# Spreading the linear layer's token blocks between attention bursts by a credit, and finishing the last block's heads through DRAM

## The chip, the cores and the metric

One core of a Trainium2 chip runs the kernel. The metric is the device time of one execution in microseconds (us); the kernel before takes 2850.27 us, the median of 3 runs (2849.86 to 2850.84). A run of this kernel can be told from no change when it differs by about 0.2%, some 6 us. TensorE does the matrix products, VectorE, ScalarE and GpSimd the element-wise work, and SyncE issues every DMA of this kernel from one queue. A profile calls these engines PE (PEld for its weight loads), DVE, ACT, POOL and SP (SPq for its queue).

## The reference: two pairs of attention layers

The input is 2048 tokens of 576 features. Layer A is attention with 32 query heads of 18 features that share one key and one value head; layer B is linear attention with learned features. They run twice, with the same weights:

```python
x = x + A(layernorm(x)); x = x + B(layernorm(x))
x = x + A(layernorm(x)); x = x + B(layernorm(x))

def A(x):   # multi-query softmax attention
    q = heads(x @ wq); k = x @ wk; v = x @ wv        # 32 x 18 queries, 18 keys, 18 values
    p = softmax(einsum("bhqd,bkd->bhqk", q, k) * 18**-0.5)
    return merge(einsum("bhqk,bkd->bhqd", p, v)) @ wo

def B(x):   # linear attention, 32 heads of 18
    q, k, v = split(x @ wqkv)
    phi = lambda t: concat(softmax(t @ w_phi), softmax(-t @ w_phi))      # 36 features a head
    kv, z = einsum("bhsf,bhsd->bhfd", phi(k), v), sum_s(phi(k))
    return merge((phi(q) @ kv) / (phi(q) @ z + 1e-6)) @ wo_b
```

Everything is float32. Since phi(k)ᵀv is a sum over all tokens, layer B can read nothing out before the last token has passed through layer A.

## The kernel before

**Stages.** The 2048 tokens are 16 blocks of 128. The program is: a setup (layer norm, queries, keys and values of the first layer A); the attention of layer 0; a bridge; the attention of layer 1; and the end. The bridge and the end finish layer B: they mix the blocks that are left, build the state `kvb` (`finish_state`) and read all 16 blocks out (`read_out`, PE line 748); the bridge also prepares the next layer's queries.

**Units.** An attention stage (`attend`) walks through 32 groups, each one block of 128 queries and half of the heads (16). A group has 16 key tiles of 128 keys, and each key tile two units of 8 heads. One unit is two score matmuls (PE line 510) into one of three PSUM tiles, and one exponential over 128 x 1024 (ACT line 988) into one of nine tiles `pt`. So there are 1024 units in a stage. The exponentials of a key tile are then multiplied with the values by four matmuls (PE line 797; the profile shows each in two passes, so 8 per key tile), summed in a PSUM bank over the group. Two banks take turns: one holds the group's sum, the other is the only spare bank, and everything else that PE does in the stage goes through it, one product at a time.

**The rest of a group.** After its last key tile `finish_group` divides by the denominators on DVE (`turned`, `osb`, `parts`, lines 907 to 915, 133 and 134) and writes the heads to DRAM (`keep_group`, `od<-parts`, 8 DMAs, line 829). After a block's second group `load_heads` reads all heads back, transposed (`on<-od`, 4 DMAs, lines 834 and 835).

**The filling work.** For each finished block `stream` gives PE two output projections (14 matmuls of 128 x 288 each, line 240; weights `wo`, input `on`), DVE adds them to the residual (`xc`, line 297), and the block is stored (`xd<-xc`). `flip_tokens` then normalizes it and sends it through DRAM to transpose it (`flipped<-pht`, `xn<-flipped`), and `split_tokens` makes `xs` of it (DVE lines 133 and 134, 664, 665). With `xs`, `mix` runs six more such projections (keys twice, values twice, queries twice, with feature maps on DVE and an exponential on ACT, line 550), and the state update (`update_state`, 32 small matmuls, line 587). So a block is 8 projections and one state update.

**The order of the work** on PE and DVE in the stage is that in which the loop at the end of `attend` records it; a list of dependencies pins it. One turn of the loop is: three units of scores, all value products that are ready, three units of scores, then one projection out of `stream` (`fill`), and again the ready value products unless the filling was long. Where `stream` waits (it sets `st["idle"]`), the loop goes in steps of two units and one key tile. A `tick` moves the generators of DVE work and weight loads one step on.

**The end of a stage.** `last_group` normalizes the last group, and `pack` moves its heads from `parts` into the transposed place `on` by 22 DMAs inside SBUF (lines 853, 856). Both output projections of block 15 wait for that. After it, all of block 15's layer norm follows, and `last_mix` mixes the blocks of `st["left"]`: three in layer 0, two in layer 1. The weights `wpq` for their queries are read again from DRAM, since the room that held them in the stage is gone.

Of the kernel before, what the change touches and what calls it, by code (L numbers as in the profile page):

```python
# [61 lines left out]
def kernel(ctx, tc, x_in, wq, wk, wv, wo, wqkv, w_phi, wob, out):  # L62
# [185 lines left out]

    def run(gen):
        for _ in gen:  # L250
            pass
# [50 lines left out]
    def fold_phi(ps, tmp):  # L302
# [33 lines left out]
        short(ps.tile([P, P], F32, name="ps"), st)  # L336
        yield -110
        for n, (half, k) in enumerate(units):
            following = fetch(n + 1)
            pt = ps.tile([P, 4, P], F32, name="ps")  # L340
# [4 lines left out]
            po = ps.tile([P, 504], F32, name="ps")  # L345
# [5 lines left out]
            pl = ps.tile([P, 2 * P], F32, name="ps")  # L351
# [210 lines left out]
    def keys_values(i, xs, e, st, ps, copies):  # L562
        vb = st["vb"][i % 2]
        for b in range(2):
            po = ps.tile([P, HALF], F32, name="ps")
            yield from project(po, st["wk"], b * HALF, xs, lambda: feature_start(heads(po), e, b, copies))
# [10 lines left out]
        for b in range(2):  # L577
            po = ps.tile([P, HALF], F32, name="ps")
            yield from project(po, st["wv"], b * HALF, xs, lambda: values(po, b))
        return vb  # L580

    def update_state(e, vb, st, ps, after=None):
        phi = e.rearrange("p h s d -> p (h s d)")
        pk = ps.tile([P, SG * 2 * DH], F32, name="ps")
# [13 lines left out]
    def queries(xs, e, st, ps, copies):  # L598
        for b in range(2):
            po = ps.tile([P, HALF], F32, name="ps")  # L600
            yield from project(po, st["wpq"], b * HALF, xs, lambda: feature_start(heads(po), e, b, copies))
# [44 lines left out]
    def flip_tokens(i):  # L646
        rstd, bias = ln_stats([i])[i]
        xn = bw.tile([P, H, 2, DH], F32, name="featq").rearrange("p h s d -> p (h s d)")[:, :D]
        V.tensor_scalar(xn, xres[i], rstd, bias, op0=ALU.mult, op1=ALU.add)
        blocks = bw.tile([P, NKG, P], F32, name="pht").rearrange("p a b -> p (a b)")  # L650
        run(block_transpose(blocks[:, :D], xn, flipped[i]))
# [16 lines left out]
    def mix(i, xs, st, ps, spill, loads, slow, after):  # L668
        ek, eq = (bw.tile([P, H, 2, DH], F32, name=tag) for tag in ("featk", "featq"))
        vb = yield from keys_values(i, xs, ek, st, ps, V)  # L670
# [10 lines left out]
    def last_mix(n, i, stats, st, sp, ps, spill):  # L681
        xn = layer_norm(i, stats, bw if n % 2 else sp, A, "xn" if n % 2 else "xo")
        yield STAGE
        xs = bw.tile([P, 9, P], F32R, name="xs") if n % 3 == 0 else sp.tile([P, 9, P], F32R, name="xs3")
        yield from transposed(xn, xs, ps, A, LOE)
        yield STAGE
        if n % 2:
            ek, eq = (bw.tile([P, H, 2, DH], F32, name=tag) for tag in ("featk", "featq"))
        else:
            both = sp.tile([P, 9, PW], F32, name="xsc").rearrange("p a b -> p (a b)")  # L690
            ek, eq = (both[:, k * 2 * D : (k + 1) * 2 * D].rearrange("p (h s d) -> p h s d", s=2, d=DH)
                      for k in range(2))
        vb = yield from keys_values(i, xs, ek, st, ps, A)
        yield STAGE
        if n < 2:
            yield from queries(xs, eq, st, ps, A)
# [3 lines left out]
        if n >= 2:  # L700
# [3 lines left out]
        pht = sp.tile([P, NKG, P], F32, name="phs", bufs=1)  # L704
# [35 lines left out]
    def read_out(i, pht, st, sp, ps):  # L740
# [22 lines left out]
        for b in range(2):  # L763
            po = ps.tile([P, HALF], F32, name="ps")
# [72 lines left out]
    def load_first_heads(on, c):  # L837
        src = ods[c % 2]
        for n in range(2):
            nc.sync.dma_start(on[:, 5 * n : 5 * n + 2, :], src[n, : 2 * P].rearrange("(k p) t -> p k t", p=P))  # L840
            nc.sync.dma_start(on[:32, 5 * n + 2, :], src[n, 2 * P : 2 * P + 32])

    def pack(dst, src, g):
        for j in range(GH):
            for x in range(HS):
                row, cols = (first_head(g, j) + x) * DH, slice(x * P, (x + 1) * P)
                d0 = 0
                while d0 < DH:
                    k, r = divmod(row + d0, P)
                    n = min(DH - d0, P - r)  # L850
                    rows = slice(32 * j + d0, 32 * j + d0 + n)
                    if k < 4:
                        nc.sync.dma_start(dst[r : r + n, k : k + 6 : 5, :], src[rows, :, cols])  # L853
                    else:
                        for half in range(2):
# [546 lines left out]
```

## Time and profile before

| | before |
|---|---|
| median of 3 runs | 2850.27 us |
| the profiled execution | 2848.92 us, of it the span 2847.1 us |
| PE / PEld busy | 2667.7 us (94%) / 1474.3 us (52%) |
| ACT busy | 2147.3 us (75%), 1920.1 us of it exponentials of scores |
| DVE / POOL busy | 1249.2 us (44%) / 61.6 us (2%) |
| DMA | 251.81 MB, mean 88 GB/s |
| mean granted clock of PE | 0.968 |

A row of the timeline has a start in us, a duration, the engine, the source line, the operation, output and input, and how many such instructions were merged; in brackets stands the idle time of the engine before it and what ended that. PE's rows overlap, because matmuls are pipelined, so the distance from the start of one group of scores to the next is the better measure of what a burst costs. In the view of waits a row says who waited for whom, how long in total, how often, and the longest. A table by stretches gives the busy time of each engine in each of them, the granted clock, the share of the DMA engines and GB/s.

### The profile page before, as it was taken

Reading aid. Unit: us, or ns where it says so; the run is one execution under the profiler, and the core shown is the slowest. Engines: PE = TensorE matmul, PEld = TensorE weight load, DVE = VectorE, ACT = ScalarE, POOL = GpSimd, SP = SyncE. Lnnn points to the kernel's source line nnn. Section 1 sums busy time; section 2 is a strip of 40 time slices with the busy share of each in tenths; the row PEclk is TensorE's granted clock in tenths of the full one; section 3 lists DMA queues with packets and bytes.
Section 4 is the critical chain, followed back from the end, with each engine's and each line's share of the span. In section 5 each row is a group of like instructions: output and inputs, shape, how many; then the busy total and the mean of one; then the engine's idle time right before and its main releaser. Section 6 shows DMA issues by size and latency. Waiting matters only on the chain. (4 is left out here: it accounts for less than half of the span.)

```text
span 2847.1 us, 55572 instructions
## 1 busy us (share of the span) xinstructions
PE 2667.7 (94%) x22046; PEld 1474.3 (52%) x22046; DVE 1249.2 (44%) x2852; ACT 2147.3 (75%) x2521; POOL 61.6 (2%) x102
## 2 busy tenths in 40 slices
PE   7999999999999999979999999999999999999799
PEld 6633434444444444538994344444444444444389
DVE  8432144444444444437772233443344443444165
ACT  4699988888988887953337888888888888888621
POOL 1000000000000000002000000000000000000010
PEclk9999999999999999989999999999999999999889
DMA  6463244222222322126546222222221222221164
GB/s 188 149 209 109 64 118 135 56 60 52 60 60 55 73 63 64 48 60 214 176 127 209 57 56 56 56 56 48 51 59 45 54 57 51 56 56 38 40 206 147
DMA packets 472596, 251.81 MB, mean 88 GB/s; under 512 B 216136, under 2 KB 426632, under 8 KB 472328
## 3 DMA queue, kind: packets, MB, share of 16 engines
q1 hardware_dynamic: 472328, 248.17, 31.3%
q8 instruction: 177, 2.90, 0.4%
q14 instruction: 91, 0.75, 0.1%
HBM read 140.90 MB, written 104.63 MB: 86 GB/s over the span
## 5 line engine op out<-in xcount | busy, mean ns | idle before, releaser
L988 ACT ACTIVATE pt<-sc 128x1024 f32<-128x1024 f32 x2036 | 1920.1, 1047 | 310.5 <-PE sc L510 294.6
L510 PE MATMUL sc<-qst,kst 56*128 56x512 f32 x3840 | 703.4, 453 | 24.9 <-ACT pt L988 22.1
L510 PEld LDWEIGHTS sc<-qst,kst 56*128 56x128 f32 x3840 | 322.6, 186 | 574.2 <-ACT pt L988 521.4
L797 PE MATMUL acc<-pt,vst 128*32 128x512 f32 x4096 | 498.6, 602 | 6.1 <-DVE xc L297 3.3
L797 PE MATMUL ps<-pt,vst 128*32 128x512 f32 x4048 | 497.0, 603 | 0.0
L240 PE MATMUL ps<-wahi,xs 128*128 128x288 f32 x1035 | 236.7, 315 | 27.5 <-DVE xs L133 23.7
L797 PEld LDWEIGHTS acc<-pt,vst 128*32 128x32 f32 x4096 | 107.3, 109 | 226.7 <-issue 214.7
L797 PEld LDWEIGHTS ps<-pt,vst 128*32 128x32 f32 x4048 | 105.9, 110 | 215.4 <-issue 210.9
L240 PEld LDWEIGHTS ps<-wahi,xs 128*128 128x128 f32 x1035 | 177.2, 197 | 55.9 <-issue 25.2
L240 PE MATMUL ps<-walo,xs 128*128 128x288 f32 x575 | 174.5, 305 | 0.0
L240 PE MATMUL acc<-wchi,on 128*128 128x288 f32 x477 | 115.4, 327 | 34.8 <-DMA on<-od 33.9
L297 DVE TENSOR_TENSOR xc<-xc,acc 128x288 f32<-128x288 f32 x53 | 23.9, 451 | 252.8 <-PE acc L240 252.8
L240 PEld LDWEIGHTS acc<-wchi,on 128*128 128x128 f32 x477 | 83.2, 202 | 59.5 <-issue 25.9
L240 PEld LDWEIGHTS ps<-walo,xs 128*128 128x128 f32 x575 | 113.6, 198 | 0.0
L388 PE MATMUL ps<-xsc,wbhi 128*128 128x256 f32 x576 | 107.0, 284 | 0.7 <-ACT xsc L131 0.7
L240 PE MATMUL ps<-wbhi,xs 128*128 128x288 f32 x486 | 107.0, 305 | 0.0
L131 ACT ACTIVATE xs<-ps 128x512 fp32r<-128x512 f32 x37 | 22.0, 595 | 107.0 <-PE ps L283 106.9
L574 DVE COPY vb<-ps 128x288 f32<-128x288 f32 x44 | 20.1, 458 | 186.2 <-PE ps L240 186.2
L410 ACT ACTIVATE pc<-ps 128x256 fp32r<-128x256 f32 x80 | 30.5, 385 | 93.6 <-PE ps L388 90.8
L907 DVE STREAM_TRANSPOSE turned<-ps 128x512 f32<-128x512 f32 x32 | 22.9, 717 | 158.4 <-PE ps L797 121.1
L388 PEld LDWEIGHTS ps<-xsc,wbhi 128*128 128x128 f32 x576 | 90.8, 191 | 1.6 <-ACT xsc L131 1.1
L240 PEld LDWEIGHTS ps<-wbhi,xs 128*128 128x128 f32 x486 | 79.6, 188 | 16.1 <-issue 15.7
(263 smaller groups left out, 3034.0 us busy)
## 6 DMA issues: line engine op xcount, KB each, us to landing
qst<-qd SPq DMA_DIRECT2D x360, 72.0 KB
od<-parts SPq DMA_DIRECT2D x496, 36.0 KB
pht<-phi SPq DMA_DIRECT2D x32, 540.0 KB
qd<-pc SPq DMA_DIRECT2D x64, 256.0 KB
phi<-pht SPq DMA_DIRECT2D x108, 144.0 KB
on<-od SPq DMA_DIRECT2D x60, 256.0 KB
xd<-xc SPq DMA_DIRECT2D x33, 288.0 KB
xc<-xd SPq DMA_DIRECT2D x30, 288.0 KB
```

What stands on the lines that cost most here:

```text
L131: A.activation(dst_hi, src, AF.Copy)
L240: T.matmul(dst, xs[:, slot, :], w[half][:, k, c0 : c0 + HALF], start=(n == 0), stop=(n == last))
L297: V.tensor_add(xr, xr, po)
L388: T.matmul(po, lhs, xsc[:, slot, :], start=(n == 0), stop=(n == LASTP))
L410: A.activation(pc[:, 0, :], po, AF.Copy)
L510: T.matmul(sc, kst[head_rows(h), t * P : (t + 1) * P], q[head_rows(h), h // 2, :], start=True, stop=True)
L574: V.tensor_copy(dst, heads(po))
L797: T.matmul(acc[32 * j : 32 * j + 32, :], vst[:, t, :], pts[j], start=first, stop=last)
L907: V.transpose(turned, acc[c, g])
L988: A.activation(pt, sc, AF.Exp, scale=SCALE)
```

## The change

**Pacing.** `bankful` lets `stream` say what its next product is before it takes the spare bank: a projection ("P"), a state update ("U") or a piece of the weights' folding ("F"). `peek` runs `stream` up to there. Each burst of three units earns credit (`PACES`: 0.6 a burst while layer 0's weights are folded, then 0.44; 0.39 in layer 1; at most 2 are held). A projection takes the place of a burst's value products, costs one credit, and never comes in two bursts in a row. Otherwise the burst has two or three key tiles of value products, and a state update stands behind them.

**A block early.** `hooks` record the layer norm's statistics and the flip of the next block between the value projections of the present one, and `turn_tokens` records its `xs` split behind the state update. `wanted` lets a block's mix start only when the output of the following block is done. `flip_tokens` normalizes in place in `xres[i]` now. After `load_heads` there are four steps of waiting instead of three.

**The end of a stage.** Two blocks are left in either layer, 14 and 15. Block 14's `last_mix` is recorded in pieces between those of `last_group`, so all its projections stand ahead of block 15's output projections. The last group's heads go the way of all others: `keep_group` to DRAM, and `load_part` back. `pack` is gone, and the order of `wo` and `wpq` in the rooms is exchanged, so that `wpq` stays to the end and is not read again.

```diff
+    def bankful(kind, ps, shape=(P, HALF)):
+        yield Kind(kind)
+        return ps.tile(list(shape), F32, name="ps")
...
-    def flip_tokens(i):
-        rstd, bias = ln_stats([i])[i]
-        xn = bw.tile([P, H, 2, DH], F32, name="featq").rearrange("p h s d -> p (h s d)")[:, :D]
-        V.tensor_scalar(xn, xres[i], rstd, bias, op0=ALU.mult, op1=ALU.add)
+    def flip_tokens(i, stats):
+        rstd, bias = stats[i]
+        V.tensor_scalar(xres[i], xres[i], rstd, bias, op0=ALU.mult, op1=ALU.add)
...
-    def pack(dst, src, g):
...
+    def load_part(on, c, g):
+        src, edge = ods[c % 2], HG * DH - 2 * P
+        for n in range(2):
+            k = 5 * n
+            if g == 0:
+                nc.sync.dma_start(on[:, k : k + 2, :], src[n, : 2 * P].rearrange("(k p) t -> p k t", p=P))
+                nc.sync.dma_start(on[:edge, k + 2, :], src[n, 2 * P : 2 * P + edge])
+            else:
+                nc.sync.dma_start(on[edge:, k + 2, :], src[n, 2 * P + edge : 3 * P])
+                nc.sync.dma_start(on[:, k + 3, :], src[n, 3 * P : 4 * P])
+                nc.sync.dma_start(on[n * 64 : n * 64 + 64, 4, :], src[n, 4 * P :])
...
-            pack(on.bitcast(F32), parts.bitcast(F32), NG - 1)
+            keep_group(parts.bitcast(F32), c, NG - 1)
+            load_part(on.bitcast(F32), c, NG - 1)
...
-                    for _ in range(3):
+                    for _ in range(4):
...
+            def burst():
+                ready = scores(BURST)
+                tick()
+                earn(BURST)
+                work = peek()
+                held = at[0] + BURST - 2 * done[0]
+                if work == "P" and credit[0] >= 1 and not paused[0] and held <= TILES:
+                    fill()
+                    credit[0] -= 1
+                    paused[0] = True
+                else:
+                    paused[0] = False
...
+                    count = 3 if credit[0] + st["pace"] >= 1 else 2
+                    sums(min(ready, max(done[0] + count, -(-(at[0] + BURST - TILES) // 2))))
+                    if work == "U":
+                        fill()
+                    tick()
...
                 if not st["idle"]():
-                    sums(scores(BURST))
-                    tick()
-                    ready = scores(BURST)
-                    spent = fill()
-                    in_order()
-                    opens = done[0] < len(units) // 2 and units[2 * done[0]][1] == 0
-                    if spent < HEAVY and not (spent and opens):
-                        sums(ready)
-                    tick()
-                    tick()
+                    burst()
...
+    PACES = ((0.6, 0.44), (0.39, 0.39))
...
-            on, c = st["on"], NT - 1
-            last_group(st["last"], on, ps)
-            EARLY, LATE = range(6), range(6, len(PRODUCTS))
...
+                on = st["heads_in"]()
+                load_part(on.bitcast(F32), c, 0)
+                ahead = last_mix(left[0], ln_stats(left[:1]), st, bw, ps, spills[layer])
+                closing = last_group(st["last"], on, c, ps, tail)
...
+                for job in (ahead, closing, ahead, closing, ahead, ahead):
+                    advance_to(job)
+                for b in range(2):
+                    po = ps.tile([P, HALF], F32, name="ps")
+                    run(project(po, st["wo"], b * HALF, on))
+                    add_residual(c, b, po)
```

**DVE at the opening of a mix, layer 1.** The order before, from the flip of a block to the first copy of its keys; `turned`, `osb` and the `parts` belong to a group that ends in between:

```order
L639 STREAM_TRANSPOSE pht<-featq 128x576
L907 STREAM_TRANSPOSE turned<-ps 128x512
L911 RECIPROCAL rd<-turned 128x16
L912 TENSOR_TENSOR turned<-turned,rd 128x512
L915 STREAM_TRANSPOSE osb<-turned 128x512
L133 CAST parts<-osb 128x512
L134 TENSOR_TENSOR parts<-osb,parts 128x512
L133 CAST xs<-xn 128x512
L134 TENSOR_TENSOR xs<-xn,xs 128x512
L664 CAST xs<-xn 128x128
L665 TENSOR_TENSOR xs<-xn,xs 64x128
L543 COPY featk<-ps 128x16x18
```

The four rows `xs<-xn` were the last thing ahead of the first key copy: the key projection that it copies had to wait for them. In the change the same four rows stand behind the state update (`kv<-kv,acc`) of the block before, ahead of the rest of the group's end:

```order
L551 COPY featq<-ps 128x16x18
L553 TENSOR_REDUCE fmax<-featq 128x16
L554 TENSOR_REDUCE fmin<-featq 128x16
L555 TENSOR_TENSOR featq<-fmin,featq 128x16x18
L556 TENSOR_TENSOR featq<-featq,fmax 128x16x18
L908 STREAM_TRANSPOSE turned<-acc 128x512
L603 TENSOR_TENSOR kv<-kv,acc 128x288
L133 CAST xs<-xn 128x512
L134 TENSOR_TENSOR xs<-xn,xs 128x512
L673 CAST xs<-xn 128x128
L674 TENSOR_TENSOR xs<-xn,xs 64x128
L912 RECIPROCAL rd<-turned 128x16
```

Between these rows and the first key copy of that block now lie two output projections and five to eight more bursts.

**PE around a state update, layer 1.** Before, from the burst behind the last query projection to the first output projection (`acc<-wchi,on`):

```order
L510 MATMUL sc<-qst,kst 128x512 x6
L797 MATMUL ps<-pt,vst 32x512 x12
L510 MATMUL sc<-qst,kst 128x512 x6
L587 MATMUL acc<-featk,vb_17415 32x36 x32
L797 MATMUL ps<-pt,vst 32x512 x4
L510 MATMUL sc<-qst,kst 128x512 x6
L797 MATMUL ps<-pt,vst 32x512 x8
L510 MATMUL sc<-qst,kst 128x512 x6
L240 MATMUL acc<-wchi,on 128x288
```

In the change, the same place:

```order
L518 MATMUL sc<-qst,kst 128x512 x6
L806 MATMUL ps<-pt,vst 32x512 x12
L597 MATMUL acc<-featk,vb_17365 32x36 x32
L518 MATMUL sc<-qst,kst 128x512 x6
L806 MATMUL ps<-pt,vst 32x512 x4
L518 MATMUL sc<-qst,kst 128x512 x4
L806 MATMUL ps<-pt,vst 32x512 x4
L518 MATMUL sc<-qst,kst 128x512 x6
L806 MATMUL ps<-pt,vst 32x512 x8
L518 MATMUL sc<-qst,kst 128x512 x6
L240 MATMUL acc<-wdhi,on 128x288
```

A two-unit step (scores x4) and its key tile now stand in addition between the group's end and the first product that needs `on`.

**PE behind the last value products of layer 1.** Before, with `acc<-pt,vst` the last products, lines 866 and 873 the transposes of `last_group`, then block 15's output:

```order
L797 MATMUL acc<-pt,vst 32x512 x12
L866 MATMUL ps<-idf,xn 128x128 x4
L873 MATMUL ps<-idf,featk 128x128 x4
L240 MATMUL ps<-wchi,on 128x288
L240 MATMUL ps<-wclo_17979,on 128x288
```

In the change (`osb` and `wide` are `last_group`'s, `xn` and `xs` are block 14's):

```order
L806 MATMUL acc<-pt,vst 32x512 x8
L864 MATMUL ps<-idf,osb 128x128 x4
L290 MATMUL ps<-idf,xn 128x128 x4
L294 MATMUL ps<-idf,xn 128x128
L873 MATMUL ps<-idf,wide 128x128 x4
L240 MATMUL ps<-wahi,xs 128x288
L240 MATMUL ps<-walo,xs 128x288
```

Block 14's six projections (84 matmuls) and its state update come next, and only then block 15's output projections.

More of the change, by code (lines that the diff above doesn't have):

```diff
@@ L1366 @@
             order = range(NT)
-            jobs = [last_mix(n, i, stats, st, sp, ps, spills[layer]) for n, i in enumerate(left)]
+            st["sp"] = sp
+            jobs = [last_mix(c, stats, st, sp, ps, spills[layer]), ahead]
             jobs += [finish_state(st, sp, ps)]
```

214 lines of the change are left out of this document (112 added, 102 removed).

## The prediction
> **What bounds the kernel now.** I first cut the span into its stages, at the first exponential and at the last value products of either attention stage. The columns are the stretch, its length, the busy time of PE, PEld, DVE, ACT and POOL, the granted clock, the share of the DMA engines and GB/s.
>
> ```profile
> span 2847.1 us, 55572 instructions
> ...
> 110.30:1251.90 1141.60, 1093.37 (x8639) 516.52 (x8639) 466.39 (x947) 996.21 (x1076) 8.12 (x15) 0.98 0.30 83
> 1251.90:1511.00 259.10, 233.96 (x2469) 223.54 (x2467) 173.44 (x511) 80.14 (x186) 25.41 (x34) 0.94 0.52 159
> 1511.00:2680.80 1169.80, 1107.20 (x8637) 517.15 (x8637) 440.40 (x888) 994.07 (x1080) 8.11 (x15) 0.98 0.24 61
> 2680.80:2847.10 166.30, 139.97 (x1604) 132.59 (x1604) 86.00 (x245) 26.28 (x60) 10.47 (x10) 0.89 0.50 153
> ```
>
> Two attention stages are 2311 us of 2847. In either ACT has about 995 us of work, so 147 and 176 us are left in which it stands; PE looks busy, but a matmul that is queued behind another counts as busy. What a burst costs is read from the timeline, where the starts of the score groups follow each other:
>
> ```profile
> 1841.39 0.90 PE L510 MATMUL sc<-qst,kst 56*128 56x512 f32 x4
> ...
> 1843.22 0.91 PE L510 MATMUL sc<-qst,kst 56*128 56x512 f32 x4
> ...
> 1848.72 2.86 ACT L988 ACTIVATE pt<-sc 128x1024 f32<-128x1024 f32 x3 [2.39 <-PE sc L510]
> ...
> 1858.09 0.96 PE L510 MATMUL sc<-qst,kst 56*128 56x512 f32 x6
> ...
> 1861.04 1.06 PE L510 MATMUL sc<-qst,kst 56*128 56x512 f32 x6
> 1862.03 2.78 PE L797 MATMUL acc<-pt,vst 128*32 128x512 f32 x24
> 1864.74 0.96 PE L510 MATMUL sc<-qst,kst 56*128 56x512 f32 x6
> ```
>
> A burst with a projection takes 2.95 us (1858.09 to 1861.04), of it 1.99 the projection, and one with three key tiles of value products 3.70: the pair is 6.65 us for six units, of which ACT needs 5.7 (two times 2.86). A two-unit step takes 1.83 us. There ACT is the limit: PE's own share is 0.32 for each unit and 0.93 for the key tile, 1.57. So PE bounds the stage where projections stand, ACT where none stand, and PE's idle 0.26 us a step is all that spreading can use.
>
> **Stalls on PE.** The waits of the layer 1 stage (ACT's, then PE's), and an opening of a mix that waits, from the timeline:
>
> ```profile
> ACT pt L988 <- PE sc L510: 167.4, 153, 6.3
> ...
> PE ps L240 <- DVE xs L133: 23.7, 13, 2.8
> PE acc L240 <- DMA on<-od: 17.1, 21, 2.0
> ...
> 1913.03 0.91 PE L510 MATMUL sc<-qst,kst 56*128 56x512 f32 x4
> ...
> 1917.32 0.37 PE L240 MATMUL ps<-wahi,xs 128*128 128x288 f32 x1 [2.38 <-DVE xs L133]
> ...
> 1920.53 1.65 PE L510 MATMUL sc<-qst,kst 56*128 56x512 f32 x6
> ```
>
> This two-unit step with the first key projection takes 7.50 us (1913.03 to 1920.53) where 1.83 + 1.99 = 3.82 would do. DVE reaches `xs` only behind a group's end, as the order of before shows. Of the 15 such openings in layer 1, eleven look like this one and four like the step that began at 1843.22 and ended with this row, 4.89 us later:
>
> ```profile
> 1848.11 0.97 PE L510 MATMUL sc<-qst,kst 56*128 56x512 f32 x6
> ```
>
> That is 11 x 3.68 + 4 x 1.07 = 45 us. The first output projection waits for the heads out of DRAM:
>
> ```profile
> 1884.79 3.28 SPq L829 DMA_DIRECT2D od<-parts  x8
> ...
> 1888.89 0.38 SPq L834 DMA_DIRECT2D on<-od  x1
> ...
> 1890.78 0.97 PE L510 MATMUL sc<-qst,kst 56*128 56x512 f32 x6
> ...
> 1893.29 0.54 PE L240 MATMUL acc<-wchi,on 128*128 128x288 f32 x2 [0.92 <-DMA on<-od]
> ...
> 1895.08 0.97 PE L510 MATMUL sc<-qst,kst 56*128 56x512 f32 x6
> ```
>
> Its burst takes 4.30 instead of 2.95 us, and about 13 of 15 do: 18 us. The trip through DRAM is 8.5 us, from the first issue at 1884.79 to the arrival at 1893.29.
>
> The wait at 1917.32 cost more than itself: 3.68 us were lost with 2.38 us of idle, since the projection took 3.21 us (1917.32 to 1920.53) instead of 1.99. The Trainium skill (TensorE: Matmul & The Clock Gate, What's actually happening) says that an idle window of about 3.4 us halves PE's clock until a busy one has passed. The row agrees in kind with a shorter gap; by the page alone a 2.38 us gap would cost 2.38 us, and the openings 14 us less.
>
> **Layer 1's stage, by bursts.** The order of the change holds the same work, 114 projections and 14 state updates, as 98 pairs (14 of them with a state update), 16 single projection bursts, 61 bursts with two key tiles, 12 with one and 77 two-unit steps. A burst with two key tiles needs 0.96 + 1.85 on PE and 2.86 on ACT, so 2.86; one with one tile 0.96 + 0.93 = 1.89. The state update is
>
> ```profile
> 1885.88 0.75 PE L587 MATMUL acc<-featk,vb 128*32 128x36 f32 x63
> ```
>
> 98 x 6.65 + 14 x 0.75 + 16 x 2.95 + 61 x 2.86 + 12 x 1.89 + 77 x 1.83 = 1048 us, and 15 for the 16 units at the start: 1063. The same sum for before (99 pairs, 15 openings at 3.82, 34 bursts with two tiles, 86 steps, 36 with one tile, 14 state updates, and the start) is 1066. So the spreading by itself gives 3 us; the 104 us by which the stage exceeds its sum are the 45 and 18 of stalls, and 41 of bursts gated by ACT where a feature exponential falls in, and of the start. In the change `xs` is split five or more bursts ahead of its first use, at least 10 us, and `on` has one step of waiting more and a further burst with two key tiles: from `osb` to its first product I count at least four two-unit steps and a burst, 10.2 us, against the 8.5 and some 1.2 of DVE. Both stalls go. What is late next is the gating by ACT: I keep 30 of the 41 (bounds 15 and 50, for new waits too). 1063 + 30 = 1093: **-77 us** (-92 to -57).
>
> **Layer 0's stage.** One block more is mixed here: six projections and a state update, + 6 x 1.99 + 0.75 = 12.7 us, on PE, which bounds it. The stalls that go:
>
> ```profile
> PE acc L240 <- DMA on<-od: 16.8, 11, 4.3
> ...
> PE acc L240 <- DVE featk L543: 5.0, 1, 5.0
> ...
> PE acc L797 <- DVE xc L297: 3.3, 1, 3.3
> ```
>
> 25.1 us of idle, which with the slow clock behind it (3.68 for 2.38) are 39. Six may stay, because weights are stored to DRAM in this stage. -33 + 13 = **-20 us** (-40 to +5).
>
> **The two ends.** The chain of waits behind the last value products of layer 1:
>
> ```profile
> 2680.83 0.70 DVE xn L863
> ...
> 2685.81 0.70 DVE xs L134
> 2686.69 0.76 SPq L856
> ...
> 2702.78 0.70 SPq L856
> ...
> 2706.16 0.88 ACT xo L273
> ...
> 2708.88 10.02 PE ps L240 x56
> 2719.45 3.73 PE ps L240 x28
> ...
> 2744.68 2.53 PE ps L748 x44
> ```
>
> And two rows of DVE's timeline in that stretch:
>
> ```profile
> 2705.55 0.94 DVE L297 TENSOR_TENSOR xc<-xc,ps 128x288 f32<-128x288 f32 x2 [19.05 <-PE ps L240]
> ...
> 2708.37 0.16 DVE L266 SCALAR_TENSOR_TENSOR lnb<-mv,rstd 128x1 f32<-128x1 f32 x1 [0.72 <-POOL rstd L264]
> ```
>
> SP issues `pack`'s 22 DMAs one by one, 17 us, and PE has next to nothing meanwhile; the first read-out comes 63.9 us after the last value products. In the change the normalization takes 5.0 to the first heads (2680.83 to 2685.81) and 1.2 more, for two DVE rows of block 14 stand ahead. Then 8.5 for the trip, and 3 for six more loads at about 0.5 each: `on` is there at 17.7. PE does block 14 in this time: from about 4 us on 84 matmuls, 10.02 + 3.73, and the state update, to 18.5. The output projections 3.7: 22.2. From then on block 15 stands alone: sum and statistics 3.0 (2705.55 to 2708.53), norm and transposes 2.7 (2706.16 to 2708.88), keys and values 8 to 10, state 2, queries 3.7, which makes 43 at the first read-out, and two of doubt for a cold PE: 45, **-19 us** (-24 to -10). The rest of the end is as before.
>
> The bridge starts its read-outs (first start in this row) 73.2 us after its last value products at 1251.9, since it mixes three blocks:
>
> ```profile
> L748 PE MATMUL ps<-kvb,pht x704: 206/222/357, 1325.1 to 1469.8; 108*64 108x57 f32 x160, 72*64 72x38 f32 x16
> ```
>
> In the change the same 45, so -28; up to 3 may be lost where read-outs wait for their output weights, whose 10 DMAs can start only after block 15's keys. **-27 us** (-32 to -15).
>
> A rule against this part: the Trainium skill (DMA: Bandwidth & Descriptors, Anatomy of one DMA) gives every DMA a fixed cost of about 2 us, mostly the receipt of the last write, and a way through DRAM pays it twice where `pack` pays once. By it the ends would be 2 us worse each; the measured trip of 8.5 us holds both.
>
> **The sum.** 2847.1 - 20 - 27 - 77 - 19 = 2704 us of span; 1.8 us lie around it (2848.92), and the median stands 1.4 above this execution: 2707.
>
> **The rivals.** First, the stalls only change their place: each new step of the chain (spare bank, DVE, DRAM) is late elsewhere, so that the stages keep their 104 and about 70 us above the sums. Layer 1 gives 3, layer 0 loses 13; with the ends -46 that is -36: about 2814. For it speaks that the sums of bursts are hardly better; against it, that the waits have known causes, which the order removes. Second, the other side: DVE now meets `xs<-xn` ahead of a group's `turned` and `osb`, and if the block is not back from DRAM, DVE stands, and behind it the group's end, `on`, and the emptying of the spare bank for which PE waits. The price is in this row of all waits:
>
> ```profile
> DVE xs L133 <- DMA xn<-flipped: 25.6, 5, 10.5
> ```
>
> 28 flips at 10.5 us are 294 us, against -143: 3001. It turns the sign from 5.1 us a flip on, just this row's mean. Against it: from flip to split lie two pairs and a state update, over 13 us, and the row has five waits in 27 flips of before. Third, ACT-gating goes too, because PE always has something in hand: the stages reach their sums and layer 0 loses all its idle, 1063 and about 1100: 2850.3 - 107 - 42 - 48 = 2653. The bursts next to two-unit steps speak against it.
>
> **How the numbers follow.** 0.70 for the forecast, 0.12 for the first rival, 0.05 for the second, 0.11 for the third, 0.02 for no change at all or less. The terms' bounds, which will not all fall on one side, make 2675 to 2745; a part of the first and third rival makes the range 2662 to 2770. Faster by over 0.2% is 0.94, slower 0.05.
>
> **What would show it.** Right: the layer 1 stage takes 1078 to 1113 us, its waits of PE for `xs` and for `on` are each under 6 us, ACT's wait for scores falls from 167 to below 110, and the first read-outs come 40 to 50 us after the last value products. The forecast is wrong if the waits vanish and the stage still takes over 1130 (then the sum by bursts is wrong), or if DVE shows long waits for `xn<-flipped` or PE for the spare bank's emptying.

## The result, and the profile after

The changed kernel takes 2770.67 us (median of 4 runs, 2763.83 to 2773.81) against 2850.56 of before on the same chips; the ratio is 0.9715, with an interval of 0.9695 to 0.9735. It is faster by 80 us, where 143 were forecast: the median lies 0.7 us beyond the upper end of the range, and the interval reaches into it. The table by stretches of the profile after, cut at the same events as that of before; a stage begins at its first scores, some 1 us ahead of the first exponential (length, busy time of PE, PEld, DVE, ACT and POOL, granted clock, DMA share, GB/s):

```profile
span 2767.5 us, 55568 instructions
...
110.80:1252.10 1141.30, 1098.64 (x8787) 526.52 (x8787) 488.07 (x988) 1000.57 (x1082) 8.12 (x15) 0.99 0.31 82
1252.10:1480.80 228.70, 217.47 (x2303) 208.46 (x2303) 162.15 (x485) 72.63 (x170) 20.64 (x30) 0.97 0.55 168
1480.80:2617.80 1137.00, 1088.46 (x8637) 517.54 (x8637) 439.27 (x886) 998.93 (x1080) 7.88 (x15) 0.98 0.24 62
2617.80:2767.50 149.70, 132.55 (x1604) 126.51 (x1604) 87.29 (x246) 26.01 (x60) 10.72 (x11) 0.97 0.53 161
```

| stretch | before | forecast | after |
|---|---|---|---|
| layer 0's stage | 1141.6 | -20 (-40 to +5) | 1141.3, -0.3 |
| bridge | 259.1 | -27 (-32 to -15) | 228.7, -30.4 |
| layer 1's stage | 1169.8 | -77 (-92 to -57) | 1137.0, -32.8 |
| end | 166.3 | -19 (-24 to -10) | 149.7, -16.6 |

Both ends came as worked out. The read-outs (first start in the row of either layer) begin 42.8 and 43.8 us behind the last value products:

```profile
L757 PE MATMUL ps<-kvb,pht x704: 206/222/357, 1294.9 to 1439.6; 108*64 108x57 f32 x160, 72*64 72x38 f32 x16
...
L757 PE MATMUL ps<-kvb,pht x704: 206/222/357, 2661.6 to 2754.4; 108*64 108x57 f32 x160, 72*64 72x38 f32 x16
```

What is missing, 64 us, lies in the two attention stages. The waits of layer 1's stage (ACT's, PE's with its weight loads, and DVE's) show where:

```profile
ACT pt L992 <- PE sc L518: 124.7, 145, 6.0
...
PE acc L240 <- DMA on<-od: 29.1, 20, 2.7
...
PEld acc L240 <- DMA on<-od: 13.3, 12, 1.7
...
DVE xs L133 <- DMA xn<-flipped: 3.8, 1, 3.8
```

PE has no wait for `xs` any more (23.7 us before), and DVE's waits for a block on its way back are 3.8 us instead of 25.6. But PE waits for `on` longer than before, 29.1 instead of 17.1 us. One such place, in the timeline:

```profile
1831.01 2.03 SPq L838 DMA_DIRECT2D od<-parts  x1
...
1838.99 1.38 DVE L649 STREAM_TRANSPOSE pht<-featq 128x1152 f32<-128x1152 f32 x1
1840.40 0.31 SPq L652 DMA_DIRECT2D phi<-pht  x1
1840.69 0.96 PE L518 MATMUL sc<-qst,kst 56*128 56x512 f32 x6
1840.88 0.48 SPq L843 DMA_DIRECT2D on<-od  x1
...
1843.97 0.37 PE L240 MATMUL acc<-wdhi,on 128*128 128x288 f32 x1 [2.31 <-DMA on<-od]
1844.17 0.29 PE L240 MATMUL acc<-wdlo,on 128*128 128x288 f32 x1
1845.48 0.85 PE L240 MATMUL acc<-wdhi,on 128*128 128x288 f32 x2 [1.02 <-DMA on<-od]
...
1847.81 0.67 PE L240 MATMUL acc<-wdhi,on 128*128 128x288 f32 x2
1848.29 0.33 PE L240 MATMUL acc<-wdlo,on 128*128 128x288 f32 x1
1848.54 0.96 PE L518 MATMUL sc<-qst,kst 56*128 56x512 f32 x6
```

The last part of the heads is issued to DRAM by 1833.04, and the first of the loads that bring them back starts only at 1840.88, 7.8 us later. Between the two, on SP, stands the first DMA that stores the block's features (`phi<-pht`), and it waits for DVE's transposition, which ends at 1840.37. In the kernel before the load followed at once (1888.89 in the prediction's row, behind eight issues that end at 1888.07). The burst takes 7.85 us (1840.69 to 1848.54) instead of 2.95.

SP's rows of the whole stage show the same order in 13 of 15 blocks. In nine of them the store's data are late, and the load starts 7.8 to 9.6 us behind the last store of heads; in eight of these PE's first product then waits 2.0 to 2.7 us. In the kernel before the store stood there in 6 blocks, and no load started more than 3.1 us behind. The 113 projection bursts of the stage, from one start of scores to the next, take 380 us instead of 113 x 2.95 = 333.

### The profile page after: what moved, and what is told of

It reads as the page before. It is cut to its first block, busy times and chain, and to the rows that moved or that the text cites. A ratio compares the mean times of both kernels' runs of the same rounds, so it can differ in the third digit from the quotient of the medians.

```text
span 2767.5 us, 55568 instructions
## 1 busy us (share of the span) xinstructions
PE 2631.2 (95%) x22030; PEld 1464.7 (53%) x22030; DVE 1259.8 (46%) x2867; ACT 2148.7 (78%) x2511; POOL 56.9 (2%) x98
## 5 line engine op out<-in xcount | busy, mean ns | idle before, releaser
L518 PE MATMUL sc<-qst,kst 56*128 56x512 f32 x3840 | 694.9, 452 | 21.2 <-ACT pt L992 20.9
L240 PE MATMUL ps<-wahi,xs 128*128 128x288 f32 x882 | 193.3, 305 | 0.8 <-ACT xs L131 0.6
L240 PEld LDWEIGHTS ps<-wahi,xs 128*128 128x128 f32 x882 | 145.9, 190 | 11.4 <-issue 7.8
L240 PE MATMUL ps<-walo,xs 128*128 128x288 f32 x490 | 144.6, 297 | 0.0
L240 PE MATMUL acc<-wdhi,on 128*128 128x288 f32 x450 | 110.0, 329 | 32.0 <-DMA on<-od 31.9
L240 PEld LDWEIGHTS acc<-wdhi,on 128*128 128x128 f32 x450 | 79.7, 205 | 51.9 <-issue 32.7
L418 ACT ACTIVATE pc<-ps 128x256 fp32r<-128x256 f32 x80 | 30.4, 384 | 94.4 <-PE ps L396 92.9
L240 PE MATMUL ps<-wbhi,xs 128*128 128x288 f32 x459 | 100.9, 305 | 0.0
L240 PE MATMUL ps<-wchi,xs 128*128 128x288 f32 x432 | 96.0, 308 | 0.0
L240 PEld LDWEIGHTS ps<-walo,xs 128*128 128x128 f32 x490 | 93.3, 190 | 0.0
L396 PE MATMUL ps<-xsc,wblo 128*128 128x256 f32 x320 | 86.5, 286 | 0.0
```

Source lines behind the costliest of these rows:

```text
L240: T.matmul(dst, xs[:, slot, :], w[half][:, k, c0 : c0 + HALF], start=(n == 0), stop=(n == last))
L396: T.matmul(po, lhs, xsc[:, slot, :], start=(n == 0), stop=(n == LASTP))
L418: A.activation(pc[:, 0, :], po, AF.Copy)
L518: T.matmul(sc, kst[head_rows(h), t * P : (t + 1) * P], q[head_rows(h), h // 2, :], start=True, stop=True)
```

## The experiments

Each ran on a chip together with the kernel before, so the ratios are to be compared; one thousandth is 2.8 us. The lengths are read from each run's profile in the same way as above. E1 to E4 start from the changed kernel, E5 to E9 from E1, E10 to E12 are as their texts say.

| run | median us | ratio (interval) | layer 0 | bridge | layer 1 | end | first read-outs |
|---|---|---|---|---|---|---|---|
| after | 2770.7 | 0.9715 (0.9695 to 0.9735) | 1141.3 | 228.7 | 1137.0 | 149.7 | 42.8, 43.8 |
| E1 feature store late | 2712.7 | 0.9539 (0.9518 to 0.9560) | 1132.0 | 229.0 | 1093.4 | 146.8 | 43.5, 43.9 |
| E2 eight steps | 2720.7 | 0.9571 (0.9549 to 0.9593) | 1137.3 | 229.0 | 1086.5 | 155.4 | 43.1, 52.6 |
| E3 guard | 2756.1 | 0.9688 (0.9664 to 0.9711) | 1136.0 | 230.3 | 1133.1 | 152.6 | 42.6, 44.7 |
| E4 block 14 behind | 2785.5 | 0.9800 (0.9777 to 0.9822) | 1138.8 | 236.3 | 1134.4 | 163.9 | 53.4, 62.1 |
| E5 no spreading | 2745.8 | 0.9653 (0.9631 to 0.9675) | 1149.9 | 230.3 | 1104.2 | 150.6 | 42.7, 42.6 |
| E6 split at use | 2726.4 | 0.9586 (0.9566 to 0.9606) | 1139.0 | 229.3 | 1097.2 | 146.0 | 43.4, 43.1 |
| E7 old folding | 2700.7 | 0.9496 (0.9475 to 0.9517) | 1100.5 | 246.8 | 1093.6 | 145.9 | 56.3, 42.8 |
| E8 slower folding | 2723.4 | 0.9573 (0.9551 to 0.9595) | 1144.5 | 229.0 | 1091.3 | 148.9 | 43.4, 44.4 |
| E9 no early flip | 2749.0 | 0.9664 (0.9635 to 0.9692) | 1141.4 | 242.8 | 1089.4 | 158.8 | 52.4, 56.6 |
| E10 old folding, six steps | 2720.0 | 0.9557 (0.9528 to 0.9585) | 1134.6 | 227.3 | 1089.5 | 157.0 | 42.3, 49.3 |
| E11 the same, pace 0.37 | 2714.1 | 0.9544 (0.9515 to 0.9573) | 1134.8 | 228.0 | 1077.8 | 160.9 | 42.3, 57.9 |
| E12 no opening behind | 2749.6 | 0.9667 (0.9651 to 0.9683) | 1112.6 | 228.7 | 1137.8 | 159.7 | 43.0, 57.5 |

**E1, the feature store eight ticks later.**

```diff
-        next(spilling)
-        slow.append(spilling)
+        slow.append(later(spilling))       # later: eight ticks, then the same job
```

> The store of a block's features (phi<-pht) is recorded eight ticks later; PE's order stays the same. Theory A (SP's queue): in the changed kernel on<-od stands on SP behind phi<-pht, which waits for DVE's transposition, so the 12 late output projections of layer 1 cost 78 us instead of 12 x 2.95 = 35. Here on<-od comes ahead of it: PE's wait for on<-od in the layer 1 stage falls from 29 us to under 6, the stage from 1137 to 1095 (1090 to 1105), layer 0's stage stays within 8 us of 1141, the time is about 2728. Theory B (the trip through DRAM is too long for the steps that cover it, whatever SP does): the wait stays over 20 us and the time within 10 us of 2771. Theory C (stalls only change their place): the wait goes, but the stage stays above 1120, with another wait of PE or ACT grown by as much.

The job that is put off holds DVE's transposition as well as the store. Layer 1's stage fell to 1093.4, the ratio by 0.0176, some 50 us. The 113 projection bursts take 337 us instead of 380, and those 43 us are all that the stage lost. PE has no wait for `on` in its list, and the timeline of the same block shows why:

```profile
1817.82 0.38 SPq L847 DMA_DIRECT2D on<-od  x1
...
1826.16 0.40 PE L240 MATMUL acc<-wdhi,on 128*128 128x288 f32 x1
...
1828.20 1.08 PE L518 MATMUL sc<-qst,kst 56*128 56x512 f32 x6
...
1835.35 1.37 DVE L649 STREAM_TRANSPOSE pht<-featq 128x1152 f32<-128x1152 f32 x1
...
1836.75 0.95 SPq L652 DMA_DIRECT2D phi<-pht  x2
```

The load starts 8.3 us ahead of its first product and not 3.1. Theory A holds. PE's order is the same, so the steps were enough to cover the trip through DRAM (against B), and no other wait took its place (against C): ACT's waits for scores fell from 124.7 us too:

```profile
ACT pt L996 <- PE sc L518: 79.2, 134, 5.7
```

**E2, eight steps in place of four.**

```diff
-                    for _ in range(4):
+                    for _ in range(8):
```

> Eight steps instead of four between load_heads and the output projections; this moves also the order of bursts, and on SP on<-od comes ahead of phi<-pht. Theories A and B both let the wait for on<-od go and the layer 1 stage fall to 1090 to 1110; B alone expects this run to gain where the one with the late feature store does not. Theory C keeps the stage above 1120. Layer 0's stage, whose waits for on are 3 us, stays within 10 us of 1141 by all. Time 2720 to 2745 by A and B.

Layer 1's stage is 1086.5. This does not show that more steps cover a late load, since no load is late here: in all 15 blocks it starts 0.8 to 0.9 us behind the last store of heads, ahead of the feature store. Nor is the whole gain one of the stage: two projections moved from it into the end, where the last block is mixed later (first read-out 52.6 us behind the last value products instead of 43.8).

**E3, the guard of the folding.**

```diff
+                    filled = work == "F" and credit[0] >= 1      # ahead of the fill
...
-                    count = 3 if credit[0] + st["pace"] >= 1 else 2
+                    opens = filled and done[0] < len(units) // 2 and units[2 * done[0]][1] == 0
+                    count = 0 if opens else 3 if credit[0] + st["pace"] >= 1 else 2
```

> Behind a folding product no value products that open a new group (the guard that the kernel before had): three bursts of layer 0 change, the rest of PE's order stays. Theory A (the -20 of layer 0 was eaten in the folding, by value products that wait for DVE to empty the bank): the three waits of PE of 2.7, 2.4 and 2.0 us at value products go, with the slow clock behind them 8 to 12 us, so layer 0's stage goes from 1141 to about 1131 and the time to about 2761. Rival (the folding is bound by DVE's copies between its products, PE merely waits for them at another place): layer 0's stage stays within 4 us of 1141. Layer 1 stays at 1137 by both.

Layer 0's stage fell by 5.3 us, half of what theory A wanted; with runs of one kernel 10 us apart that decides nothing by itself. Of the three waits that it was to remove, two went and the one of 2.0 us stayed. This is one of the two, in the changed kernel:

```profile
333.39 0.66 PE L350 MATMUL ps<-idf,wstage 128*126 128x128 f32 x4
...
335.45 0.69 DVE L134 TENSOR_TENSOR parts<-osb,parts 128x512 fp32r<-128x512 f32 x1
336.06 0.68 DVE L351 COPY xn<-ps 126x512 f32<-126x512 f32 x1
...
336.79 1.94 PE L806 MATMUL ps<-pt,vst 128*32 128x512 f32 x8 [2.74 <-DVE xn L351]
```

A folding product sits in the spare bank, DVE has a group's end ahead of the copy that empties it, and the value products behind it need that bank, since they open a new group.

**E4, block 14 behind the last output.**

```diff
-                for job in (ahead, closing, ahead, closing, ahead, ahead):
+                for job in (closing, closing):
```

> Block 14's keys, values and queries go behind block 15's output projections, as in the kernel before; the heads still go through DRAM. Theory A (block 14 fills the 14 us in which PE would wait for the last heads): in either end the first read-out comes 10 to 15 us later (53 to 58 us behind the last value products instead of 43), the time is 2790 to 2800. Rival (block 14's products would lie beside block 15's chain of small steps anyway): the read-outs start within 4 us of 43, the time within 8 us of 2771. The attention stages stay as they are by both.

The first read-outs came 10.6 and 18.3 us later, the second by more than the 15 that theory A allowed, and the ratio rose by 0.0085, 24 us. Block 14's 14 us of products do fill the wait for the last heads; behind block 15's chain they are not hidden.

**E5, no spreading.**

```diff
-    PACES = ((0.6, 0.44), (0.39, 0.39))
+    PACES = ((0.6, 9), (9, 9))
```

> On the kernel with the late feature store (2712.7 us), the pace is so high that credit never holds a projection back behind the folding: projections come in every second burst and the rest of a block's time is two-unit steps, 115 instead of 77 of them in layer 1. Theory A (the sum of bursts decides, spreading by itself is worth 3 us): layer 1's stage by the same prices is 114 x 2.95 + 101 x 3.70 + 14 x 4.45 + 16 x 2.86 + 12 x 1.89 + 115 x 1.83 + 15 = 1066, against 1063, so 1093 becomes 1096 (1086 to 1106), and the time 2712 to 2725. Theory B (spreading is what takes the stalls away): waits for xs and on return, the stage is 1125 or more, the time above 2745.

Layer 1's stage is 1104.2, within theory A's bounds; 4.7 us of it is one wait of value products for DVE. Layer 0's stage grew by 18, which neither theory had, and which took the time beyond theory A's 2725: there the waits of value products for `xc` are 9.1 us against 1.7 in E1. Spreading is worth little by the sum of bursts. That it also keeps projections off the places at which DVE is late is a reading of these waits and was not tried by itself.

**E6, the split at its use.**

```diff
-                        yield from mix(i, parts, st, ps, spills[layer], loads, slow, hooks(), turn_tokens)
+                        turn_tokens()                        # ahead of the mix
+                        yield from mix(i, parts, st, ps, spills[layer], loads, slow, hooks(), None)
```

> On the kernel with the late feature store, xs is split where its block begins and not behind the state update of the block before; PE's order is the same, and 208 of 2823 rows of DVE's order move. Theory A (the early split is what took the waits for xs away): PE waits for xs again at about 14 openings in either layer, 1 to 3.7 us each, layer 1's stage goes from 1093 to 1107 to 1140, the time to 2740 to 2790. Theory B (the burst that credit puts between the last output projection and the first key projection, and the group's end that no longer stands there, cover the split): waits for xs stay under 5 us, the time within 10 us of 2713.

Of some 28 openings three wait for `xs`, 3.8 us each, one in layer 1 (the row below) and two in layer 0. The early split is worth about 0.0047, 13 us, and is not what took the 15 waits of before away; the time lies just outside the 10 us that theory B allowed.

```profile
PE acc L240 <- DVE xs L133: 3.8, 1, 3.8
```

**E7, the old turn in the folding.**

```diff
+                if not st["idle"]() and st["folding"]:
+                    sums(scores(BURST)); tick()
+                    ready = scores(BURST)
+                    work = peek()
+                    if work: fill()
+                    opens = done[0] < len(units) // 2 and units[2 * done[0]][1] == 0
+                    if work != "P" and not (work and opens): sums(ready)
+                    tick(); tick()
```

> On the kernel with the late feature store, the folding of layer 0's weights runs in the turn of the kernel before (every second burst of value products makes room for a folding product or a projection, no credit); behind it the credit's bursts as they are. By bursts layer 0's stage keeps its sum within 5 us, with 13 instead of 38 two-unit steps. Theory A (layer 0's missing gain lies in stalls of the folding: PE waits 17 us for DVE there against 4.5 before, about 18 with the slow clock): layer 0's stage goes from 1132 to 1110 to 1118, the time to about 2695. Theory B (what is gained in the folding is paid later, since the blocks come in fewer and denser bursts): layer 0's stage stays within 6 us of 1132. Layer 1 stays at 1093 by both.

Layer 0's stage is 1100.5, but one projection and a state update (one projection fewer than E10's expectation counts) ran over into the bridge, whose first read-out now stands 56.3 us behind the last value products. Counted to that read-out, 1210.98 + 56.3 = 1267.3 against 1242.19 + 43.5 = 1285.7 in E1: 18.4 us, as theory A has it. It is the fastest kernel of the study: 2700.7 us, by the ratios 62 less than the changed one.

**E8, a slower folding**, with the guard of E3.

```diff
-    PACES = ((0.6, 0.44), (0.39, 0.39))
+    PACES = ((0.55, 0.44), (0.39, 0.39))
```

> On the kernel with the late feature store, the guard against value products that open a group behind a folding product, and the folding's pace 0.55 instead of 0.6 credits a burst. Theory A (stalls of the folding): two or three waits of 2 to 2.7 us go, and folding products follow each other less closely, so layer 0's stage falls by 8 to 14 us from 1132, and the time to about 2702. Theory B (no gain since later bursts become denser): within 4 us of 2713.

Both theories failed: layer 0's stage is 12.5 us longer than in E1. The folding's waits shrank, but others of the same kind came behind output projections and feature copies:

```profile
PE acc L810 <- DVE xc L304: 8.1, 2, 5.1
PE ps L810 <- DVE featk L551: 4.9, 2, 4.7
```

**E9, no block ahead.**

```diff
-                    return xs is not None and (xs[0] + 1 not in st["left_out"] or xs[0] == NT - 2 or v.left() < TAIL)
+                    return xs is not None
```

> On the kernel with the late feature store (2712.7 us), a block's mix begins as soon as its xs is there, not only behind the next block's output; so there is no finished block to flip during a mix, and each block goes output, flip, eight steps, split, mix, as in the kernel before. Theory A (flipping a block early is what layer 1's gain needs): the openings wait for xs again, 15 x up to 3.7 us, layer 1's stage goes from 1093 to 1115 to 1140. Theory B (eight steps cover the trip and the split; the early flip only exchanges waits that the credit's rest covers anyway): layer 1's stage stays within 10 us of 1093; PE's waits for xs under 5 us. Layer 0 behaves in the same way, so the time is 2745 to 2790 by A and 2700 to 2725 by B.

Layer 1's stage is 1089.4, without a wait for `xs`: in the stage theory B holds, though two projections and a state update now stand behind it. The time is 36 us worse by ratio all the same, as A had it for another reason. The last blocks are mixed later, and the first read-outs come 9 and 13 us later; and layer 0's stage is 9 us longer, with 11.2 us of waits for `xc` against 1.7 in E1.

**E10, E11, E12, towards a better version.** E10 is the changed kernel with E7's folding and the first two edits; E11 has layer 1's pace 0.37 besides; E12 is E10 with layer 0's pace 0.48 and the rest:

```diff
-                    for _ in range(4):
+                    for _ in range(6):
-    PACES = ((0.6, 0.44), (0.39, 0.39))
+    PACES = ((0.6, 0.46), (0.39, 0.39))
...
+                opens = done[0] < len(units) // 2 and units[2 * done[0]][1] == 0
-                if work == "P" and credit[0] >= 1 and not paused[0] and held <= TILES:
+                if work == "P" and credit[0] >= 1 and not paused[0] and held <= TILES and not opens:
-                    if work == "F" and credit[0] >= 1:
+                    if work == "F" and credit[0] >= 1 and not opens:
```

> A version to beat both: the changed kernel with the old turn in the folding, six steps behind load_heads instead of four (so that the feature store, at its old place, is covered by steps), and layer 0's pace 0.46, with which the last mixed block ends inside the stage. Layer 0's stage: 1100.5 of the run with the old folding, plus two projections and a state update that ran over there, about 1107; the bridge then 229 to 233 instead of 247; layer 1's stage 1086 to 1095 if on<-od comes in time, 1110 or more if the four of 14 blocks in which the feature store still stands ahead of on<-od wait. Time 2685 to 2700, in the second case 2705 to 2715.

> The same with layer 1's pace 0.37 instead of 0.39: 55 two-unit steps instead of 79, 111 bursts with two key tiles instead of 66, and on<-od ahead of the feature store in all 14 blocks. By the sum of bursts layer 1's stage is the same within 8 us; if spreading by itself gains (the run without it was 11 us slower in layer 1 and 18 in layer 0, against 3 by the sum), it is 3 to 6 us faster than with 0.39. Layer 0 and the bridge are as in the run with 0.46 and six steps.

> The version with the old folding and six steps, and with it no projection or folding product of the credit's bursts where the value products behind it would open a group; layer 0's pace 0.48, so that the last mixed block still ends inside the stage. Theory A (layer 0 loses its time where value products wait for the bank that DVE empties late: 13.9 us of idle in three waits for xc in the run with six steps, some 20 with the slow clock): those waits fall below 3 us, layer 0's stage goes from 1134.6 to 1108 to 1120, the time to 2690 to 2705. Theory B (the wait only moves to the next product that takes the bank): layer 0's stage stays above 1128, the time above 2710. Layer 1's stage stays between 1078 and 1092 by both.

E10's layer 1 came as expected, 1089.5. In four of its blocks the load still starts 8.7 us behind the last store of heads, and PE does not wait for it: here the six steps cover a late load. But its layer 0 missed its number by 28 us, and its end is 10 us longer than E1's. For layer 0 one row of waits, of which two places take 6.5 us each, gives the likely reason; this is one of the two:

```profile
PE acc L806 <- DVE xc L304: 13.9, 3, 6.5
```

```profile
694.03 0.74 DVE L563 TENSOR_REDUCE fz<-featq 128x32 f32<-128x576 f32 x1
...
697.83 1.38 DVE L649 STREAM_TRANSPOSE pht<-featq 128x1152 f32<-128x1152 f32 x1
699.13 0.42 DVE L304 TENSOR_TENSOR xc<-xc,acc 128x288 f32<-128x288 f32 x1
699.23 2.32 SPq L652 DMA_DIRECT2D phi<-pht  x4
699.60 2.79 PE L806 MATMUL acc<-pt,vst 128*32 128x512 f32 x12 [6.53 <-DVE xc L304]
```

The addition that empties the bank stands on DVE behind a block's feature sums and transposition. E12 lets no product stand there, and layer 0's stage is 1112.6 with all its work inside and without such waits: theory A in the stage, though the time missed its 2705. (E12's pace differs too, so the 22 us against E10 are not of one edit alone.) Its layer 1, which nobody expected to move, is back at 1137.8, and that is E1's mechanism once more, on four blocks:

```profile
PE acc L240 <- DMA on<-od: 41.9, 8, 9.9
```

```profile
2013.31 0.35 SPq L88 DMA_DIRECT2D xc<-xd  x1
...
2027.75 0.31 SPq L652 DMA_DIRECT2D phi<-pht  x1
2028.17 0.52 SPq L843 DMA_DIRECT2D on<-od  x1
...
2031.19 0.58 PE L240 MATMUL acc<-wdhi,on 128*128 128x288 f32 x1 [9.80 <-DMA on<-od]
```

SP stands from 2013.66 to 2027.75 before the feature store, with the heads' loads behind it. E11's stage of 1077.8 is the shortest of layer 1, but three projections and a state update moved out of it, and its end is 14 us longer than E1's. A kernel with E12's layer 0 and E1's layer 1 was not run.

## Why the prediction was right or wrong

**The sign and the ends: right.** The bridge's -30.4 and the end's -16.6 stand beside -27 and -19, and E4 shows that the step "PE does block 14 in this time" carries 24 us of these 47. The chain inside came as worked out too: at the end block 15's output projections start at 2634.71, 16.9 us behind the last value products, where 17.7 was counted. The rule of the Trainium skill (DMA: Bandwidth & Descriptors, Anatomy of one DMA) by which the prediction would make either end 2 us worse is not decided by this: its 2 us are less than the two ends' distances from the forecast, and the section's figure is a fit for DMAs that GpSimd issues, while SP issues those of this kernel.

**The size: 80 us of the 143.** Layer 1's -32.8 lies outside the bounds given for it, layer 0's -0.3 inside, but without the gain that was forecast. The bounds of the sum's terms ended at 2745. That the time still lies at the edge of the range, at 2770, owes nothing to the sum: the range reached so far only for a part of the first and third rival.

**Layer 1: the step that failed is "`on` has one step of waiting more ... I count at least four two-unit steps and a burst, 10.2 us, against the 8.5 and some 1.2 of DVE. Both stalls go."** The cover was counted on PE and DVE and not on SP. In the changed order the feature sums and the transposition stand on DVE, and so the feature store on SP, between the heads' way out and their way back. The load of the heads stands behind the store, so the way back began 7.8 us behind the way out, where it was 0.8 in the kernel before. The Trainium skill (DMA: Bandwidth & Descriptors, Anatomy of one DMA) says that a DMA's wait for a semaphore happens on the issuing sequencer before dispatch; the rows at 1831.01 to 1840.88 agree. Which edit of the change brought this order about was not tried. With the store and its transposition moved, E1 gives 1093.4 where the forecast had 1093, with the prices per burst as they were worked out (113 projection bursts at a mean of 2.98 us) and with 30 us of excess over the sum. The 30 were a choice between 15 and 50, so an agreement to the microsecond is luck. One sum has a slip: the terms given for the kernel before add up to 1064 and not 1066, so spreading gains 1 us by the sum and not 3; the forecast does not rest on it.

**The `xs` waits: gone as forecast, the reason only in part.** The forecast put it down to the early split. E6 shows that this is worth 13 us, and E9 that layer 1 has no such wait even without the early flip. All these runs share that no projection is recorded into a two-unit step, as the 15 openings of before were; that this is the cause was not tried by itself.

**Layer 0: the step that failed is "The stalls that go", 25.1 us of idle priced at 39, with at most six to stay.** The term was sized from the waits of before alone. Of those, `on` fell from 16.8 us to 2.8, but value products' waits for `xc` went from 3.3 to 4.5, and the folding was not costed at all. Before, its costliest row among PE's waits was:

```profile
PE ps L330 <- DVE featk L354: 2.5, 6, 0.8
```

Now it brought more stalls of its own; in the list of PE's waits in the stage (the rows with `featk L362`, `xn` and `featk L357` are the folding's):

```profile
PE ps L337 <- DVE featk L362: 6.4, 6, 2.6
PE acc L806 <- DVE xc L304: 4.5, 2, 2.7
PE acc L240 <- DMA on<-od: 2.8, 4, 0.8
PE ps L806 <- DVE xn L351: 2.7, 1, 2.7
...
PE acc L806 <- DVE featk L357: 2.4, 1, 2.4
PE acc L806 <- DVE xn L338: 2.0, 1, 2.0
```

The kernel before had a guard against value products that open a group behind a folding product, and the change drops it; the removed lines of the diff showed that. E7 shows the folding to be worth 18 us, and E1's layer 0 is 9 us shorter, which together is more than the 20 that were missing. E12's stage, with all its work inside, is 29 us below that of before, so the -20 was there to be had.

**The rivals.** The first, "the stalls only change their place" (2814), was half right: a stall did come back, at the place that the forecast had ruled out. The second, DVE standing before `xs<-xn`, did not happen: 3.8 us in one wait. The third, that the gating by ACT goes too, did not come either: ACT still waits 79.2 us for scores in E1's layer 1. Of the five signs named, two held (PE's waits for `xs`, the read-outs) and three spoke against the forecast: the 1137 us, ACT's 124.7 us, and the 29.1 us of waits for `on`, which named the place.

## What to carry to other kernels

When work is moved earlier, follow each of its steps onto every queue, the DMA issuer's too: here a store that waited for its data held up the loads behind it, though the loads' own data were there: in E1 the load starts 1.2 us behind the heads' last store, where it was 7.8. Of a bank or buffer that is shared, ask what stands on the emptying engine between its last use and the next; a projection or a folding product in front of a group's opening cost some 0.2 us in most places here, and 2.0 to 6.5 us where the emptying engine had other work first. A forecast made of waits that vanish should list, for each edit, what new wait could stand at the same place, and look at removed guards first.

## What was not expected of the hardware

The slow clock comes with a lag, and an idle gap of 2 to 3 us can be enough for it. In the burst at 1843.97, after 2.31 us of idle, the first two matmuls still take 0.37 and 0.29 us; those behind the second wait, from 1846.37 on, take 0.67 for two where E1 has 0.43. The granted clock of the trace says the same: 1.00 from 1841.53 to 1844.92, in which PE was busy for 0.62 of 3.39 us, then 0.50 from 1844.94 to 1848.33, and 1.00 again. So 3.33 us of idle cost 4.9. The opening that the prediction shows, with one gap of 2.38 us in the kernel before, looks alike: 1.00 from 1915.33 to 1918.72 with PE busy for 1.27 of 3.39 us, then 0.50 from 1918.74 to 1922.13.

The Trainium skill (TensorE: Matmul & The Clock Gate, What's actually happening) describes an idle window of some 3.4 us that runs freely. The stretches at half clock agree with that length; but in both cases PE was not idle through the window ahead, only for more than half of it.

In the changed kernel seven of the eight blocks whose `on` is waited for are followed by 3.4 or 6.8 us at half clock, 34 us together, and E1 has none behind the start of its stage: from 1495.6 to 2564.6 its mean is 1.00. With 29.1 us of waits for `on` and half of the 34 as an estimate of what the clock cost, 46 us, the 47 by which the 113 bursts exceed their price are nearly accounted for.
